# Attention, MoE and gated MLP in one kernel: the last token tile's logits with tokens in rows, its ranks from one-hot rows, the capacity branch ahead of the row loads, and full-size row transposes

## The chip, the cores and the metric

The kernel runs on one core of one Trainium2 chip. The metric is the device time of one execution in microseconds (us); the kernel before takes 963.38 us, the median of three runs (962.12 to 964.65). The core has five engines with a queue of instructions each: PE (TensorE, matrix products and transposes), DVE (VectorE), ACT (ScalarE), POOL (GpSimd) and SP (SyncE, which in this kernel issues nearly all DMAs). PE's weight loads have rows of their own in the profile (PEld). A "q" behind an engine's name (SPq, PEq, PEldq) marks what its sequencer does: branches, register loads, semaphore waits, DMA issues.

## The reference, cut to what matters

Three layers, each on the output of the one before. All inputs and outputs are fp32.

```python
# 1. attention: q, k, v (4, 8, 576, 64), s (4, 8, 576)
cum  = np.cumsum(np.maximum(s, 0), axis=-1)
sc   = q @ k.T / 8 + np.minimum(-(cum[:, :, :, None] - cum[:, :, None, :]), 0)   # causal mask
attn = exp(sc - max(sc)); out = attn / (sum(attn) + 1e-9) @ v
x    = out.transpose(0, 2, 1, 3).reshape(2304, 512)

# 2. mixture of experts: 8 experts, each token goes to one
logits     = normalised(x) @ normalised(expert_emb).T / tau
expert_idx = np.argmax(logits, axis=1); gate = softmax(logits)[token, expert_idx]
for e in range(8):
    out[expert_idx == e] = gate * (np.maximum(x[expert_idx == e] @ w1[e], 0) @ w2[e])   # 512 -> 1024 -> 512

# 3. gated MLP: w_a, w_b (512, 1536), w_out (1536, 512)
return ((out @ w_a) * (out @ w_b)) @ w_out
```

## The kernel before, in words

**Attention.** There are 4 batches with 4 head pairs each, so 16 units. `att` is a pool that holds this stage's buffers; `class Sched` is a planner that merges several streams of work items (scores, transposes of the exponentials, products with V, and the token-tile items below) into one order for PE by estimated due times, and puts the DVE, ACT and POOL operations (`V.push`, `V.chain`) where its model of each engine has room. What it emits is a fixed order for each engine; at run time each engine only waits on semaphores.

**Token tiles.** The 2304 tokens are 20 tiles (`NT`), five for each batch: four of 128 tokens and one of 64 tokens; in the last batch the 64-token tile is number 19, the last of all. For each tile three kinds of items follow each other. `x_item` forms the raw logits (before the softmax denominators are applied) for each head with the experts in rows (L857, the result `lp`, copied to `lt`), transposes the attention output so that tokens are in rows (L862), takes the reciprocal `r` of the denominators (L880, L887) and scales the rows (L895, the result `x`). `l_item` transposes `lt` back to tokens in rows (L930), scales it by `r` (L938, `lw`), sums over the heads (L947, `lg`), takes the maximum and its index (L950, L953), and forms the one-hot row `oh` (L956). POOL adds `oh` to a running count `sc` (L961). `r_item` gets each token's rank within its expert: a matmul of `oh` with a triangle matrix `ltri` (L982) and a matmul of the counts of the earlier tiles with `ones` (L983); DVE picks the rank (L989, L995) and makes the target row `sl` (L998), and POOL scatters the tile's rows into the DRAM buffer `xs`, sorted by expert (L1004). Ahead of the last `r_item` and behind the count matmul stand small matmuls with no use but to keep PE running (`warm`, L174): 28 and 30 of them (`WARM[5]`, `WARM[2]`).

**Counts.** Behind the last tile PE sums `sc` (L1250), and DVE sorts the experts by their counts: a chain of some 15 small operations from L1257 on. L1268 finds by how much the largest expert exceeds its capacity, and L1274 casts all these numbers to the integers `ci` that the sequencers load as registers. Each expert slot has a capacity in rows (`CAPS`: 352 for slot 0, and between 272 and 368 for the others).

**Between the stages.** The order from here on is written out by hand:

```python
            xload(0)
            wload2()
            for _ in range(4):
                misc.pop(0)()
            cbase[1] = nc.sync.value_load(ci[:1, 1, 1:2], min_val=0, max_val=N)
            ...                                     # 30 warm matmuls
            most = nc.values_load(ci[:1, 2, 0:1], min_val=-CAP, max_val=N)
            overflow()
            zfill(1)
```

`xload(0)` (L1332, L1333) loads slot 0's rows from `xs` into `xg`; it waits for all scatters. `misc` is a list of small DVE and ACT steps (the gate, output positions) that nothing needs until the end of the expert stage. `overflow` is a block for tokens beyond the capacity: all five engines compare `most` with zero and jump over it (L1661) when no expert overflows, as is the case here. `zfill(e)` (L1215) writes zeros into the part of `xs` that slot e's load reads beyond its rows, and `zero(xs[:CAPS[0]])` does that for slot 0 at the start of the kernel.

**Experts.** For each of the eight slots, eight steps f of 128 hidden columns: 12 matmuls `h` (L1510), then 12 matmuls `y` (L1535) for the step before. Each operand is split into a high and a low part, so three products make one. In steps 3 to 6 the next slot's rows are transposed for the next pass (`xtr`, L1361; for slot 0 `xtr0`, L1345): three transposes in each of four groups, and the third covers only the rows beyond 256 (96 rows for slot 0, 112 for slot 1, 88 and 72 for slots 2 and 3, then 40, 32, 32 and 16). `xload(e)` and `zfill(e)` run one slot ahead, on SP. Results go to `yt`.

**Third layer.** Six groups of 384 tokens. `yload(i)` (L1580) loads a group from `yt` into the same `xg` buffer, `ysplit` splits it (L1587, L1588), `tick` (among others L1433, on POOL) splits its weights, and `abmm` (L1600) and `omm` (L1621) are the products.

## Time and profile before

| | kernel before |
|---|---|
| median of 3 runs | 963.38 us (962.12 to 964.65) |
| the profiled execution | 960.65 us, its span 959.0 us |
| PE busy | 925.7 us, 97% of the span |
| DVE, ACT, POOL busy | 514.6, 432.8 and 255.1 us (54%, 45%, 27%) |
| mean granted TensorE clock | 0.994 |
| DMA | 107.90 MB, mean 113 GB/s |

The span is the time from the first to the last instruction; 1.65 us of the profiled execution lie outside it. Attention runs until about 258 us of the span, the stretch between the stages from there to 273 us, the experts to about 490 us, and the third layer to the end. A granted clock of 1.00 is 2.4 GHz, one of 0.50 is 1.2 GHz.

### The profile page before, as it was taken

Reading aid. Unit: us, or ns where it says so; the run is one execution under the profiler, and the core shown is the slowest. Engines: PE = TensorE matmul, PEld = TensorE weight load, DVE = VectorE, ACT = ScalarE, POOL = GpSimd, SP = SyncE. Lnnn points to the kernel's source line nnn. Section 1 sums busy time; section 2 is a strip of 40 time slices with the busy share of each in tenths; the row PEclk is TensorE's granted clock in tenths of the full one; section 3 lists DMA queues with packets and bytes.
Section 4 is the critical chain, followed back from the end, with each engine's and each line's share of the span. In section 5 each row is a group of like instructions: output and inputs, shape, how many; then the busy total and the mean of one; then the engine's idle time right before and its main releaser. Section 6 shows DMA issues by size and latency. Waiting matters only on the chain.

```text
span 959.0 us, 17720 instructions
## 1 busy us (share of the span) xinstructions
PE 925.7 (97%) x6471; PEld 846.6 (88%) x6472; DVE 514.6 (54%) x1319; ACT 432.8 (45%) x1075; POOL 255.1 (27%) x311
## 2 busy tenths in 40 slices
PE   8999999999889999999999999999999999999996
PEld 7777778777779999999998999999999999999995
DVE  8688889798764334444558888742222212222112
ACT  6677788876745444455544444432211211211111
POOL 6122323256223333344302433642001001001001
PEclk9999999999999999999999999999999999999999
DMA  4774555526286667667645443613010010000000
GB/s 130 172 155 110 137 119 124 139 71 183 72 254 227 225 192 231 201 211 222 190 156 166 132 132 119 108 18 100 1 33 34 1 33 33 1 1 33 1 1 33
DMA packets 102243, 107.90 MB, mean 113 GB/s; under 512 B 58429, under 2 KB 72717, under 8 KB 102141
## 3 DMA queue, kind: packets, MB, share of 16 engines
q1 hardware_dynamic: 98557, 97.04, 36.2%
q0 software_dynamic: 3552, 9.46, 2.8%
q8 instruction: 65, 1.06, 0.5%
q14 instruction: 37, 0.30, 0.1%
q10 hardware_dynamic: 32, 0.04, 0.0%
HBM read 77.90 MB, written 20.44 MB: 103 GB/s over the span
## 4 chain that ended last, share of the span: by engine, by line
PE 66%; DVE 2%; DMA 2%; issue 1%; ACT 0%; POOL 0%; POOLq 0%; SPq 0%; DVEq 0%; ACTq 0%
PE h L1600 15%; PE x L1600 15%; PE y L1621 13%; PE h L1510 11%; PE y L1535 10%; PE x L1361 1%; DMA xg<-xs 1%; PE x L1621 1%; PE h L1621 1%; DMA xg<-yt 1%; DVE cv L262 0%; DVE cv L265 0%; DVE mx L1611 0%; DVE w L1433 0%; DVE xl L1588 0%
## 5 line engine op out<-in xcount | busy, mean ns | idle before, releaser
L1611 DVE TENSOR_TENSOR mx<-x,mx 128x384 f32<-128x384 f32 x72 | 40.0, 556 | 220.0 <-PE x L1600 220.0
L1612 ACT CAST hh<-mx 128x384 fp32r<-128x384 f32 x71 | 36.4, 513 | 161.1 <-DVE mx L1611 161.1
L1606 ACT COPY mx<-h 128x384 f32<-128x384 f32 x72 | 34.6, 481 | 144.1 <-PE h L1600 144.1
L650 ACT ACTIVATE z<-z,mn 128x192 f32<-128x192 f32 (+3 forms) x128 | 78.2, 611 | 37.8 <-DVE mn L644 37.2
L1640 POOL DMA_INDIRECT out_dram<-mx,pmt x18 | 17.6, 979 | 291.0 <-DVE mx L1639 221.7
L1600 PE MATMUL x<-xh,w 128*128 128x384 f32 x288 | 79.0, 335 | 1.0 <-POOL w L1433 1.0
L1600 PE MATMUL h<-xh,w 128*128 128x384 f32 x288 | 79.7, 337 | 0.0
L1600 PE MATMUL h<-xh,v 128*128 128x384 f32 x288 | 79.7, 337 | 0.0
L630 PE MATMUL st<-KS,QS 128*128 128x288 f32 (+3 forms) x160 | 58.6, 374 | 8.9 <-DVE mn L644 7.5
L738 PE MATMUL pt<-ident,z 128*128 128x128 f32 x448 | 63.4, 277 | 3.2 <-ACT pT L180 1.6
L1519 DVE SCALAR_TENSOR_TENSOR hl<-h,hh 128x288 fp32r<-128x288 f32 (+6 forms) x64 | 31.2, 488 | 65.1 <-ACT hh L1518 65.1
L280 POOL TENSOR_TENSOR w<-st,w 128x512 fp32r<-128x512 f32 (+1 forms) x41 | 44.5, 1093 | 74.2 <-ACT w L272 48.9
L644 DVE CUSTOM_DVE_ANT_0 z<-st,maskb 128x192 f32<-128x192 f32 (+3 forms) x128 | 58.7, 478 | 9.5 <-PE st L633 7.6
L782 PE MATMUL xa<-pT,vn 128*64 128x128 f32 x896 | 61.2, 282 | 0.8 <-ACT pT L180 0.4
L1613 DVE TENSOR_TENSOR hl<-mx,hh 128x384 fp32r<-128x384 f32 x71 | 39.7, 559 | 41.1 <-ACT hh L1612 41.1
L1621 PE MATMUL y<-v,hh 128*128 128x512 f32 x192 | 59.8, 392 | 0.0
L280 POOL TENSOR_TENSOR v<-st,v 128x512 fp32r<-128x512 f32 x32 | 42.9, 1341 | 63.3 <-ACT v L272 53.0
L738 PEld LDWEIGHTS pt<-ident,z 128*128 128x128 f32 x448 | 49.8, 141 | 11.0 <-ACT z L650 4.3
L1510 PE MATMUL h<-xh,v 128*128 128x256 f32 (+2 forms) x256 | 59.2, 305 | 0.0
L1510 PE MATMUL h<-xh,w 128*128 128x288 f32 (+3 forms) x256 | 58.9, 306 | 0.0
L1535 PE MATMUL y<-hh,v 128*128 128x256 f32 (+2 forms) x256 | 58.1, 300 | 0.0
L782 PEld LDWEIGHTS xa<-pT,vn 128*64 128x64 f32 x896 | 49.1, 139 | 9.9 <-issue 5.7
(299 smaller groups left out, 2525.7 us busy)
## 6 DMA issues: line engine op xcount, KB each, us to landing
st<-in_moe_w_dram SPq DMA_DIRECT2D x64, 512.0 KB
QS<-sp SPq DMA_DIRECT2D x62, 128.0 KB
st<-in_moe_w_a_dram SPq DMA_DIRECT2D x12, 512.0 KB
st<-in_moe_w_b_dram SPq DMA_DIRECT2D x12, 512.0 KB
st<-in_moe_w_out_dram SPq DMA_DIRECT2D x12, 512.0 KB
xg<-yt SPq DMA_DIRECT2D x6, 768.0 KB
xg<-xs SPq DMA_DIRECT2D x8, 512.0 KB
kn<-in_k_dram SPq DMA_DIRECT2D x24, 128.0 KB
```

The lines of the kernel that those rows point to most:

```text
L280: e.tensor_tensor(out=o[:, 1, a:b], in0=t[:, a:b], in1=o[:, 0, a:b].bitcast(F32), op=ALU.subtract)
L630: nc.tensor.matmul(st[:m, :wp], lhsT=qs[:, h, s0 - 64:s0 - 64 + m], rhs=ks[:, h, c0:c0 + wp], start=True, stop=False)
L644: nc.vector.tensor_tensor_reduce(out=z[:m, h, c0:c0 + w], in0=st[:m, :w], in1=maskb[:m, S - kk + c0:S - kk + c0 + w], op0=ALU.add, op1=ALU ...
L650: nc.scalar.activation(out=z[:m, h, :kk], in_=z[:m, h, :kk], func=AF.Exp, scale=-1.0, bias=m1, accum_out=rsum[:m, tid(b, c), 2 * p + h:2 * ...
L738: nc.tensor.transpose(out=pt[:, 128 * x:128 * x + 128], in_=zs[i][:, h, a0:a0 + 128] if c else z0s[u % 2], identity=ident)
L782: nc.tensor.matmul(xa[64 * h:64 * h + 64, :m], lhsT=v_[:m, 2 * p + h, :], rhs=locs[i][bk, h], start=bk == 0, stop=bk == c,)
L1510: nc.tensor.matmul(ph[:, :n], lhsT=w[:, hl, 128 * f:128 * f + 128], rhs=mv[:, d, :n], start=k_ == 0, stop=k_ == 11,)
L1535: nc.tensor.matmul(ys[e][d][:, :n], lhsT=w[:, hl, c0 + 128 * d:c0 + 128 * d + 128], rhs=mv[:, :n], start=f == 0 and k_ == 0, stop=f == 7 a ...
L1600: nc.tensor.matmul(p, lhsT=w[:, hl, d, c0:c0 + 128], rhs=mv[:, d, :], start=d == 0 and k_ == 0, stop=d == 3 and k_ == 2,)
L1611: nc.vector.tensor_tensor(out=g, in0=pp[1], in1=g, op=ALU.mult)
L1613: nc.vector.tensor_tensor(out=gl, in0=g, in1=gh.bitcast(F32), op=ALU.subtract)
L1621: nc.tensor.matmul(ots[i][t], lhsT=st[:, 128 * t:128 * t + 128], rhs=w[:, hl, c0:c0 + 512], start=f == 0 and k_ == 0, stop=f == 11 and k_ ...
```

## The change

1. **The last tile's logits.** For tile 19 the logit matmul takes the operands the other way round, so that `lp` comes with tokens in rows. The copy to `lt` and the transpose back (L930) fall away. Its reciprocals `r` are pushed as soon as the last four units' sums are there, and the scaling of its rows (`fx`) is pushed only behind its one-hot row.
2. **Ranks of the last batch.** POOL's running count stops at tile 15. The ranks of tiles 15 to 19 and the final count are sums of one matmul on `sc` and one on each earlier one-hot row of the batch.
3. **Branch ahead of the row loads.** DVE casts the overflow number by itself into a new tile `cov`, directly behind L1268; the sequencers load it and take the branch before `xload(0)` is issued. `xload(0)` is three DMAs instead of two. The four `misc` steps, three operations that sort the bases (`eq`, `base`) and the low parts of three weight tiles move behind the branch.
4. **Fewer warm matmuls.** 10 instead of 28 ahead of the last ranks, and 2 ahead of the branch plus 3 behind it instead of 30; these five read their operands as plain fp32 (before: the split type fp32r).
5. **Full-size transposes.** All row transposes take 128 rows, whatever the slot's rows are; for slot 0 the unused rows of the tile are set to zero.
6. **Third layer's start.** `yload(0)` is issued behind step (6, 7) instead of (7, 1); in the last slot a `tick` also runs at step 5, with another argument from step 4 on.
7. **Zeros for slot 0.** `zero(xs[:CAPS[0]], 0)` leaves the list `pend` and is emitted at the scheduler's step 14.

How this moves instructions is shown at three places. First DVE at the last tile (line numbers of after are some 34 higher here: L938, L947, L956, L895 are L972, L981, L990, L919). Before:

```order
L956 TENSOR_SCALAR oh<-iota_85,ixs 128x8
L880 TENSOR_SCALAR r<-rsum_76 64x4 x2
L887 RECIPROCAL r<-r 64x8
L989 TENSOR_TENSOR jk<-pt,oh 128x8
L895 TENSOR_TENSOR x<-pt,r 64x512
L995 TENSOR_REDUCE rk<-jk 128x1
L938 TENSOR_TENSOR lw<-pt,r 64x64
L998 SCALAR_TENSOR_TENSOR sl<-ixs,rk 128x1
L947 TENSOR_REDUCE lg<-lw 64x8
L950 MAX mx<-lg 64x8
L953 MAX_INDEX ixs<-mx,lg 64x8
L956 TENSOR_SCALAR oh<-iota_85,ixs 64x8
```

After:

```order
L990 TENSOR_SCALAR oh<-iota_85,ixs 128x8
L972 TENSOR_TENSOR lw<-pt,r 64x64
L981 TENSOR_REDUCE lg<-lw 64x8
L1031 TENSOR_TENSOR jk<-pt,oh 128x8
L984 MAX mx<-lg 64x8
L1037 TENSOR_REDUCE rk<-jk 128x1
L987 MAX_INDEX ixs<-mx,lg 64x8
L1040 SCALAR_TENSOR_TENSOR sl<-ixs,rk 128x1
L990 TENSOR_SCALAR oh<-iota_85,ixs 64x8
L919 TENSOR_TENSOR x<-pt,r 64x512
L1031 TENSOR_TENSOR jk<-pt,oh 128x8
L1037 TENSOR_REDUCE rk<-jk 128x1
```

The last tile's `lw` now stands directly behind tile 18's `oh`, and the scaling of its rows (`x`) behind its own `oh`.

Second SP, from the last weight load of the attention stage to the branch and what follows it. Before:

```order
L1332 DMA xg<-xs 128x2x512
L1333 DMA xg<-xs 96x512
L242 DMA st<-in_moe_w_dram 128x2x512
L1711 TENSOR_LOAD ci
L1711 ISA x2
L1320 TENSOR_LOAD ci
L1320 ISA x2
L1719 TENSOR_LOAD ci
L1719 ISA x2
L1661 COMPARE_AND_BRANCH
```

After, the part up to the branch, and then the part where the branch lands:

```order
L243 DMA st<-in_moe_w_dram 128x1024
L243 DMA st<-in_moe_w_dram 128x2x512 x4
L1760 TENSOR_LOAD cov
L1760 ISA x2
L1704 COMPARE_AND_BRANCH
```

```order
L1704 UNCONDITIONAL_BRANCH
L1372 DMA xg<-xs 128x512 x2
L1372 DMA xg<-xs 96x512
L1763 TENSOR_LOAD ci
L1763 ISA x2
L1356 TENSOR_LOAD ci
L1356 ISA x2
L1257 ISA
L1257 DMA xs<-zrow 736x1x256
```

The loads of slot 0's rows (`xg<-xs`) and two register loads have moved from ahead of the branch to behind it, in front of the zero fill (`xs<-zrow`).

Third SP at the end of the expert stage, around the first load of the third layer's rows (`xg<-yt`) and the last slot's register load (`ci`) and result stores (`yt<-mx`). Before, where that load stands behind several of the last slot's stores:

```order
L1547 DMA yt<-mx 128x288
L1494 UNCONDITIONAL_BRANCH
L1547 ISA
L1547 DMA yt<-mx 128x288
L248 DMA st_8900<-in_moe_w_out_dram 128x1024
L1580 DMA xg<-yt 128x4x384
```

After:

```order
L249 DMA st_8730<-in_moe_w_b_dram 128x2x512
L1623 DMA xg<-yt 128x4x384
L1537 UNCONDITIONAL_BRANCH x2
L249 DMA st_8792<-in_moe_w_b_dram 128x2x512
L1586 TENSOR_LOAD ci
L1586 ISA x2
L1537 UNCONDITIONAL_BRANCH
L1590 REGISTER_ALU
L1590 DMA yt<-mx 128x288
```

That load now stands ahead of the last slot's register load and of all its stores.

The diff, cut to its core:

```diff
-WARM = (30, 84, 30, 0, 20, 28)
+WARM = (30, 84, 2, 0, 20, 10, 3)
...
+                        n0[0] += u > last - NP
+                        if n0[0] == NP:
+                            rlast[0] = sm.tile([128, H], F32, name="r")
+                            ...
+                            V.push(t, "D", 560, f3)
...
+                        if t == NT - 1:
+                            nc.tensor.matmul(lp[:m, 32 * p:32 * p + 32], lhsT=xw, rhs=ew, start=True, stop=True)
+                        else:
+                            nc.tensor.matmul(lp[32 * p:32 * p + 32, :m], lhsT=ew, rhs=xw, start=True, stop=True)
...
+                        if t < NT - 5:
+                            V.push(t_, "G", 163, f7, lambda t2: setattr(ot, "t", t2))
...
-                    nc.tensor.matmul(rp[:, :w], lhsT=ltri, rhs=oh[:, o, :].rearrange("p t e -> p (t e)"), start=True, stop=False)
-                    nc.tensor.matmul(rp[:, :w], lhsT=ones, rhs=sc[:, o, :].rearrange("p t e -> p (t e)"), start=False, stop=True)
+                    a = min(t0, NT - 5)
+                    nc.tensor.matmul(
+                        rp[:, :w], lhsT=ones, rhs=sc[:, a:a + k_, :].rearrange("p t e -> p (t e)"), start=True, stop=False
+                    )
+                    for x in range(a, t0):
+                        nc.tensor.matmul(rp[:, :w], lhsT=ones, rhs=oh[:, x, :], start=False, stop=False)
+                    nc.tensor.matmul(rp[:, :w], lhsT=ltri, rhs=oh[:, o, :].rearrange("p t e -> p (t e)"), start=False, stop=True)
...
             nc.vector.max(out=over, in_=key)
+            nc.vector.tensor_copy(out=cov, in_=over[:1])
...
+                if e == 0:
+                    for a in range(3):
+                        m = min(128, CAPS[0] - 128 * a)
+                        behind("xs", nc.sync.dma_start(out=t[:m, a], in_=xs[128 * a:128 * a + m, :]))
+                    return
...
-                    m = min(128, cap - 128 * a)
                     nc.tensor.transpose(
-                        out=pt[:, 128 * a:128 * a + m], in_=xgs[e][:m, a, 128 * d:128 * d + 128], identity=ident[:m, :m]
+                        out=pt[:, 128 * a:128 * a + 128], in_=xgs[e][:, a, 128 * d:128 * d + 128], identity=ident
                     )
...
+            w = slots[0, 0][:, 0, :].bitcast(F32)
...
+            wload2()
+            idle(WARM[2])
+            most = nc.values_load(cov[:1, 0:1], min_val=-CAP, max_val=N)
+            overflow()
             xload(0)
-            wload2()
-            for _ in range(4):
-                misc.pop(0)()
             cbase[1] = nc.sync.value_load(ci[:1, 1, 1:2], min_val=0, max_val=N)
             who(1)
...
+            idle(WARM[6])
             count(0)
-            most = nc.values_load(ci[:1, 2, 0:1], min_val=-CAP, max_val=N)
-            overflow()
+            for j in range(4, 7):
+                for x in range(2):
+                    lo_op("DG"[j == 6], wstate[j], slots[0, j], 512 * x, 512 * x + 512)
+            for _ in range(2):
+                misc.pop(0)()
             zfill(1)
...
-                    if (e, f) == (E - 1, 1):
+                    if (e, f) == (E - 2, 7):
                         yload(0)
...
-                        for _ in range(TICKS[0] if f not in (4, 5, 6) else 0):
-                            tick(5 if f < 7 else 3)
+                        for _ in range(TICKS[0] if f not in (4, 6) else 0):
+                            tick(5 if f < 4 else 3)
```

`idle(n)` runs n `warm` matmuls of 512 columns.

## Rows read from the trace of the kernel before

**Rows 1.** Page: chain of work that ended last, share of the span by engine
```profile
PE 66%; DVE 2%; DMA 2%; issue 1%; ACT 0%; POOL 0%; POOLq 0%; SPq 0%; DVEq 0%; ACTq 0%
```

**Rows 2.** Timeline of PE: start us, us, engine line op tile xcount [idle before <-releaser]
```profile
55.50 0.88 PE L782 MATMUL xa<-pT,vn 128*64 128x128 f32 x12 [0.43 <-ACT pT L180]
...
270.21 1.06 PE L1345 MATMUL y<-ident,xg 128*128 128x128 f32 x8 [2.90 <-PEq L1661]
...
285.96 0.41 PE L1361 MATMUL x<-ident,xg 128*128 128x128 f32 x2 [0.27 <-DMA xg<-xs]
286.53 0.31 PE L1361 MATMUL x<-ident,xg 112*128 112x112 f32 x1 [0.15 <-DMA xg<-xs]
...
489.31 0.39 PE L1535 MATMUL y<-hl,v 128*128 128x256 f32 x1 [0.94 <-DVE hl L1519]
...
525.87 0.62 PE L1600 MATMUL x<-xh,w 128*128 128x384 f32 x2 [0.97 <-POOL w L1433]
```

**Rows 3.** Line L1661, the branch: durations ns min/median/max, first to last start us
```profile
L1661 SPq EVENT_SEMAPHORE  x9: 17/17/17, 270.1 to 270.7; - x9
...
L1661 PEldq COMPARE_BRANCH  x1: 5480/5480/5480, 264.4 to 264.4; - x1
L1661 SPq COMPARE_BRANCH  x1: 50/50/50, 266.5 to 266.5; - x1
```

**Rows 4.** Windows: stretch, us, busy PE PEld DVE ACT POOL, clock, DMA share, GB/s
```profile
265.00:266.00 1.00, 1.00 (x6) 0.82 (x5) 1.00 (x2) 0.00 (x0) 0.00 (x0) 1.00 1.03 369
...
273.10:275.90 2.80, 2.80 (x12) 2.80 (x13) 0.67 (x3) 0.48 (x2) 0.00 (x0) 0.50 0.89 185
```

**Rows 5.** Chain in order of time, expert stage: start us, us, what, instructions
```profile
278.03 8.45 DMA xg<-xs
...
290.06 0.32 PE x L1361 x3
290.37 1.60 PE h L1510 x12
291.97 1.58 PE y L1535 x12
...
377.61 0.40 PE x L1361 x3
378.01 2.01 PE h L1510 x12
380.02 1.82 PE y L1535 x12
...
468.97 0.38 PE x L1361 x3
469.35 1.63 PE h L1510 x12
470.98 1.44 PE y L1535 x12
```

**Rows 6.** Timeline of DVE, last tile to the overflow number
```profile
256.38 0.30 DVE L956 TENSOR_SCALAR oh<-iota,ixs 128x8 bf16<-128x8 f32 x1
...
257.82 0.20 DVE L938 TENSOR_TENSOR lw<-pt,r 64x64 f32<-64x64 f32 x1
...
258.82 0.22 DVE L956 TENSOR_SCALAR oh<-iota,ixs 64x8 bf16<-64x8 f32 x1
...
259.33 0.17 DVE L989 TENSOR_TENSOR jk<-pt,oh 128x8 f32<-128x8 f32 x1 [0.29 <-PE pt L983]
...
261.59 0.17 DVE L1268 MAX8 pk<-jk 128x8 f32<-128x8 f32 x1
```

**Rows 7.** Line L1711, SP's load of one register, columns as in rows 3
```profile
L1711 SPq TENSOR_LOAD <-ci x1: 494/494/494, 264.4 to 264.4; - x1
```

**Rows 8.** Timeline of SP, the next DMA behind the branch
```profile
271.14 0.66 SPq L1215 DMA_DIRECT2D xs<-zrow  x1
```

**Rows 9.** Timeline of ACT, first use of the third layer's rows
```profile
485.25 0.51 ACT L1587 CAST xh<-xg 128x384 fp32r<-128x384 f32 x1 [2.32 <-DMA xg<-yt]
```

More of the change, by code (lines that the diff above doesn't have):

```diff
@@ L206, in moe_kernel @@
         ci = rt.tile([1, 5, E], I32, name="ci")
+        cov = rt.tile([1, E], I32, name="cov")
         tie = rt.tile([128, E], F32, name="tie")
@@ L598, in start @@
                             pend.pop(0)()
+                if i == 14:
+                    zero(xs[:CAPS[0], :], 0)
                 if wq and i >= 5 * 12:
@@ L705, in th1, with th2, f3 @@
                         rel.t = t
-                        V.push(t, "A", 0.833 * 64 + 280, f2, lambda t2: setattr(et, "t", t2))
+                        V.push(t, "A", 0.833 * 64 + 280, f2, th2)
+                    def th2(t):
+                        et.t = t
+                        n0[0] += u > last - NP
+                        if n0[0] == NP:
+                            rlast[0] = sm.tile([128, H], F32, name="r")
+                            def f3(_):
+                                for h in range(2):
+                                    first_r(rlast[0], B - 1, h)
+                                nc.vector.reciprocal(out=rlast[0][:64], in_=rlast[0][:64])
+                            V.push(t, "D", 560, f3)
                     V.push(end, "D", 1.042 * 64 + 77, f1, th1)
@@ L838, in tid, with first_r @@
                 return 5 * b + (4 - c if b == B - 1 else c)
+            rlast, lend = [None], [None]
+            def first_r(r, b, h):
+                nc.vector.tensor_scalar(
+                    out=r[:64].rearrange("p (a h) -> p a h", h=2)[:, :, h],
+                    in0=rsum0[64 * h:64 * h + 64, NP * b:NP * b + NP],
+                    scalar1=1e-9, scalar2=None, op0=ALU.add,
+                )
             def x_item(b, c):
@@ L928, in emit @@
                     x, r, lt = rts[t]
-                    lp = ps_t.tile([128, 512], F32, name="pt")
-                    nc.tensor.transpose(out=lp[:m, :128], in_=lt[:, :m], identity=ident)
-                    rel = Tok()
-                    pts.append(rel)
+                    if t == NT - 1:
+                        lp, (rel, more) = lt, lend[0]
+                    else:
+                        lp = ps_t.tile([128, 512], F32, name="pt")
+                        nc.tensor.transpose(out=lp[:m, :128], in_=lt[:, :m], identity=ident)
+                        rel = Tok()
+                        pts.append(rel)
                     lw = sm3.tile([128, H, E], F32, name="lw")
@@ L1249, in moe_kernel @@
             pt = ps_t.tile([128, 512], F32, name="pt")
-            nc.tensor.matmul(pt[:, :E], lhsT=ones, rhs=sc[:, NT, :], start=True, stop=True)
+            nc.tensor.matmul(pt[:, :E], lhsT=ones, rhs=sc[:, NT - 5, :], start=True, stop=False)
+            for t in range(NT - 5, NT):
+                nc.tensor.matmul(pt[:, :E], lhsT=ones, rhs=oh[:, t, :], start=False, stop=t == NT - 1)
             sbase, scnt, over, perm, more = (pk[:, x] for x in range(5))
@@ L1460, in m5 @@
             def m5():
+                eq = gp.tile([128, E, E], F32, name="eq")
+                nc.vector.tensor_tensor(
+                    out=eq, in0=perm.unsqueeze(1).to_broadcast([128, E, E]),
+                    in1=iota8.unsqueeze(2).to_broadcast([128, E, E]), op=ALU.is_equal,
+                )
+                nc.vector.tensor_tensor(out=eq, in0=eq, in1=sbase.unsqueeze(1).to_broadcast([128, E, E]), op=ALU.mult)
+                nc.vector.tensor_reduce(out=base, in_=eq, axis=AX.X, op=ALU.add)
                 nc.vector.tensor_tensor(out=lt, in0=oh, in1=base.unsqueeze(1).to_broadcast([128, NT, E]), op=ALU.mult)
```

68 lines of the change are left out of this document (29 added, 39 removed).

## The prediction

> **What bounds the kernel now.** PE is busy 97% of the span, and the page's chain of work that ended last [rows 1] is two thirds PE; DMA and DVE have 2% each. So a time can be won in two ways only: PE has less to do, or a gap of PE goes. I read the timeline of PE next, for its idle times [rows 2]. Behind the attention stage there are four places: 2.90 us ahead of the first row transpose at 270.21, put down to PE's own sequencer at L1661, the capacity branch; 0.27 and 0.15 us at slot 1's transposes at 285.96, for the rows from `xs`; 0.94 us at 489.31; and 0.97 us at 525.87. The line of the branch [rows 3] shows what a branch costs there: PE's record at 264.4 lasts 5480 ns; SP's record lasts 50 ns, but its next event stands 3.6 us later, at 270.1, and the last of its nine semaphore events at 270.7. The windows [rows 4] show the DMA engines full at that time (369 GB/s, share 1.03), and PE at half its clock (0.50, that is 1.2 GHz) from 273.1 to 275.9, at the first products behind the gap. The chain in order of time [rows 5] shows two more things. The 8.45 us from 278.03 are the load of slot 1's rows, on the path to the gap at 285.96. And the row transposes cost more than their own 0.3 to 0.4 us: the `h` group behind them is longer too.
>
> **Full-size transposes (−4.1 us).** In [rows 5] the group at 347.12, whose third transpose has 72 rows, takes 0.28 us, and the `h` group behind it 1.89 where a plain group of this slot takes 1.84: 0.33 in all. The first group with 40 rows (377.61) takes 0.40, its `h` 2.01 against 1.82 behind it: 0.59. The last, with 16 rows (468.97): 0.38, and 1.63 against 1.44, so 0.57. There are 16 such groups (slots 4 to 7, with 40, 32, 32 and 16 rows), all on the path since PE is full there. A transpose of 72 rows costs no step, one of 40 does: with 128 rows I expect the 0.33. The saving is between 0.24 and 0.26, and some 16 × 0.255 = 4.1 us. The more columns cost next to nothing: 0.28 us is for 72 rows, 0.32 at most if each row beyond costs as much as those within. Bounds: 0, if the dearer step has another cause than the row count, to −4.2.
>
> **The stretch between the stages (−1.3 us).** Worked along the path that ends at slot 1's rows.
> Last tile [rows 6]: `lw` stands at 257.82 and now directly behind tile 18's `oh` of 256.38, so at about 256.57, and `oh` of tile 19 follows 1.0 to 1.2 us later, at 257.75 instead of 258.82. The scaling of its rows, some 0.6 us, then stands on DVE between this `oh` and the rank picks; PE's rank matmuls run beside it, for which DVE waited about 0.3 us before. So the count chain begins some 0.8 us earlier, the overflow number is there at 260.8 instead of 261.59, and `cov`, one small cast, at 261.0. The five matmuls more in the ranks and in the count are short and stand where 18 warm ones fall away.
> Branch: one register load takes 0.49 us [rows 7], with its checks 0.9 to the next. SP now loads one ahead of the branch, so it branches at about 261.9 instead of 266.5 [rows 3]. Before, the time from SP's branch to the next DMA issue, the zero fill at 271.14 [rows 8], was 4.6 us: 3.6 of waiting, some 0.6 of semaphore events and the setting up. Now the same wait meets fewer loads, since slot 0's rows are issued behind it and only weights ahead. No row shows it without load: the bounds are 0.5 us (the branch record and nothing more) and 5.5 (PE's record). I take 3.15, a little under SP's own; with the semaphores the row loads are issued at 265.75.
> Rows: 352 rows of 2 KB at 369 GB/s take 2.0 us; with the latency and a weight load of 512 KB in the queue (1.4 us at that rate) I put the landing 4.0 us behind the issue. Only then may the zero fill of slot 1 go, at 269.8 instead of 271.14: −1.3. From there the chain is as before (zero fill, slot 1's row loads, 8.45 us), so slot 1's rows arrive 1.3 us earlier.
> PE has to be there as early. Before, it waited for the branch until 269.9 (264.4 and 5.48) and started at 270.21. Now it branches at about 262 and, with a wait of 4 to 5.5 us, returns at 266 to 267.5; the three fp32 warm matmuls of 512 columns come then. No row has such a one; they cost 3 × 0.25 us if they run as the fp32r ones do, and 3 × 0.9 if fp32 goes in four passes. So PE is free at 269 to 270, when the rows land. The second pass of transposes no longer waits for DVE, whose `misc` steps come later, and the 0.42 us of gaps at 285.96 are left as slack. That covers the −1.3; if PE's clock drops already in the warm matmuls, some 0.9 of it are lost. Range of this part: −4.4 (wait of 0.5) to +1.0 (wait of 5.5).
> What moves behind the branch (two `misc` steps, the `eq` operations, the low parts of the weights) goes to DVE and POOL, which are busy half and a quarter of the span; the low parts are needed only by the later products of slot 0, so I cost them at nothing. If that cover is gone, PE waits some tenths of a us at slot 0's fifth weight tile.
> Here the Trainium skill speaks against the value that I took. Advanced Engine Details and Errata, Control Flow Timing, gives about 108 ns for a compare-and-branch. PE's record is fifty times as long, so I don't follow it; by it the sum would be near the lower bound above. Runtime: NRT & Kernel Launch, Instruction fetch mechanics, says that a taken branch out of the loaded pages forces a DMA fetch; the 3.6 us of [rows 3] beside full DMA engines agree with it.
>
> **Third layer's start (−1.9 us).** At 485.25 ACT waits 2.32 us for the third layer's rows `xg<-yt` [rows 9]; behind that wait stand the casts of the last slot's hidden columns, for which DVE's `hl` and then PE wait at 489.31 (0.94), and weight splits, for which PE waits at 525.87 (0.97) [rows 2]. With `yload(0)` issued ahead of the last slot's stores the rows are there, and the additional `tick` at step 5 takes one weight split forward. I take both gaps: −1.9. Bounds: −0.5 (half of one goes, since a new tick on ACT and POOL stands in the same place) to −1.9.
>
> **Zeros for slot 0 and the rest (−0.4 us).** The zero fill leaves SP's queue ahead of the next unit's loads. PE's gap of 0.43 us at 55.50, at the first use of `vn` [rows 2], stands behind such a load: I take it, with bounds 0 and −0.4. Fewer copies, one transpose less and no running count on POOL in the last batch are beside PE's work and cost nothing.
>
> **The rivals.**
> Quick branch: without the row loads in front the wait is 0.5 us. Then the middle part gives −4.4, in all −10.8: 952.6. Only the 50 ns of SP's own record speak for it; the 5480 ns of PE speak against it [rows 3].
> Slow branch: the wait is 5.5 us, for the weights alone fill the queues. Middle part +1.0, in all −5.4: 958.0.
> The gaps of the third layer stay: the ticks' order and not the load sets them. In all −5.8: 957.6.
> The change doesn't do what it says: the dearer step is not the row count's. In all −3.6: 959.8.
> Slower, by the clock: PE now has 5 warm matmuls where it had 30 and is idle from about 262 to 266 and more, where it had run until 267. Before, after an idle time of 2.90 us, half speed followed for at least 2.8 us [rows 2, 4]. If half speed now lasts through four of slot 0's steps, it costs the time of these once more: a step is 24 matmuls of 288 columns, 2 × 1.44 us at least as in slot 6 [rows 5], so 4 × 2.9 = 11.5, and 967.2. It decides from some 11 us on, that is when nearly all four are slow. The one stretch seen is short, and PE then has work without a pause, which speaks against it. The Trainium skill, TensorE: Matmul & The Clock Gate, Why this matters for your kernels, warns of idle gaps between bursts of matmuls for the same reason; the 0.50 of [rows 4] agrees.
>
> **How the numbers follow.** −4.1 − 1.3 − 1.9 − 0.4 = −7.7 us. The profiled execution took 960.65, so 952.95; the median of the runs is 2.73 above it, at 963.38, so 955.7 for the median of the changed kernel. Chances: forecast 0.60 (its own range 953.7 to 957.7), quick branch 0.09, slow branch 0.12, third layer's gaps stay 0.09, row count not the cause 0.06, clock 0.04. The range takes in all but the last, with the spread of the runs: 952.3 to 959.9. A measurement of this kernel can tell about 0.3%, 2.9 us, from no change: faster means below 960.5, slower above 966.3. Of the cases all but the last two lie well below 960.5; with the row count's case near the edge and several misses at once that makes 0.89 faster, 0.07 the same and 0.04 slower.
>
> **What would show it.** Right: transposes of slots 4 to 7 with groups of 0.33 us in all instead of 0.57 to 0.59; no gaps at the last `y` groups and at the third layer's first products; the zero fill of slot 1 issued 1 to 2 us earlier, and SP's first event behind the branch some 3 us after it. Wrong: `h` groups behind the transposes still 0.2 us longer; SP or PE standing at the branch for 5 us and more; a granted clock of 0.50 in the windows of slot 0's products for more than 5 us; or a new gap of PE in slot 0, at weight tiles whose low parts now come later.

## The result, and the profile after

The changed kernel takes 954.96 us (median of 4 runs, 953.78 to 956.2) where the kernel before takes 963.56 (962.12 to 964.65): a ratio of 0.9912, 95% interval 0.9894 to 0.993. The prediction was 955.7 with a range of 952.3 to 959.9. The profiled execution of the changed kernel takes 953.78 us with a span of 952.1, so 6.9 us less than that of before (span 959.0); the medians lie 8.6 us apart, since the profiled execution of before is 2.7 us under its median and that of after 1.2 us.

| | before | after |
|---|---|---|
| median | 963.56 us | 954.96 us |
| span of the profiled execution | 959.0 us | 952.1 us |
| PE busy | 925.7 us | 917.8 us |
| mean granted TensorE clock | 0.994 | 0.994 |

That is not the whole result. The experiments below ran on two chips on which the kernel before takes 968.2 and 970.6 to 971.0 us (which chip the first measurement ran on is not on record). On the second of them the changed kernel, repeated twice, was no faster than before (1.001 and 0.9995); on the first it was not run itself. Where its gain went, and how it comes back, is the second half of the experiments.

The timeline of PE after, at the places of [rows 2]; columns as there:

```profile
54.12 0.88 PE L800 MATMUL xa<-pT,vn 128*64 128x128 f32 x12 [0.43 <-ACT pT L180]
...
251.22 0.66 PE L800 MATMUL xa<-pT,vn 128*64 128x128 f32 x8 [1.14 <-ACT pT L180]
...
264.54 3.63 PE L174 MATMUL h<-w 128*128 128x512 f32 x4 [2.84 <-PEq L1704]
...
268.89 1.37 PE L1382 MATMUL y<-ident,xg 128*128 128x128 f32 x8
...
284.27 0.41 PE L1397 MATMUL x<-ident,xg 128*128 128x128 f32 x2 [1.25 <-DMA xg<-xs]
285.00 0.33 PE L1397 MATMUL x<-ident,xg 128*128 128x128 f32 x1 [0.32 <-DMA xg<-xs]
...
503.00 0.44 PE L1643 MATMUL h<-xh,w 128*128 128x384 f32 x1 [1.25 <-ACT mx L1649]
```

The gaps of 0.94 and 0.97 us in the third layer are gone, and one of 1.25 has come at 503.00. The gap at slot 1's transposes has grown from 0.42 to 1.57 us. The gap of 0.43 at the use of `vn` is still there, 1.38 us earlier in the span.

The chain of waits in order of time, after: start us, us, what, instructions.

```profile
266.21 3.38 DMA xg<-xs
...
269.80 6.20 DMA xs<-zrow
...
276.73 8.23 DMA xg<-xs
...
376.08 0.33 PE x L1397 x3
376.40 1.79 PE h L1553 x12
378.19 1.79 PE y L1578 x12
...
463.65 0.33 PE x L1397 x3
463.98 1.44 PE h L1553 x12
465.42 1.44 PE y L1578 x12
```

The groups of slots 4 to 7 have lost their step: 0.33 us and nothing in the `h` group behind, where [rows 5] have 0.40 with 2.01 against 1.82, and 0.38 with 1.63 against 1.44. The stretch between the stages ends in three DMAs one behind the other: the last of slot 0's row loads, the zero fill, and the last of slot 1's row loads.

The line of the branch after, columns as in [rows 3]:

```profile
L1704 SPq EVENT_SEMAPHORE  x9: 17/17/17, 263.8 to 264.4; - x9
...
L1704 PEldq COMPARE_BRANCH  x1: 3402/3402/3402, 260.8 to 260.8; - x1
...
L1704 SPq COMPARE_BRANCH  x1: 50/50/50, 261.1 to 261.1; - x1
```

**Ledger of the two profiled executions**, from the start times of the same instructions:

| stretch | before | after | won in it | forecast |
|---|---|---|---|---|
| start to tile 18's one-hot row on DVE (L956, now L990) | 256.38 | 255.54 | 0.84 | 0.4 |
| from there to the third transpose for slot 1 | 286.53 | 285.00 | 0.69 | 1.3 |
| from there to the first plain `h` group behind the last transposes | 472.42 | 466.86 | 4.03 | 4.1 |
| from there to the last result's operation on DVE | 950.80 | 943.92 | 1.32 | 1.9 |
| sum | | | 6.88 | 7.7 |

The 0.84 of the first line isn't the change's own. At the same PE instructions, PE ran at half its clock in the profile of before and at full clock after (windows: stretch, us, busy PE PEld DVE ACT POOL, granted clock, DMA share, GB/s). Before:

```profile
28.00:29.00 1.00, 1.00 (x12) 1.00 (x10) 0.48 (x2) 0.69 (x2) 0.00 (x0) 0.50 0.24 57
```

After:

```profile
28.00:29.00 1.00, 1.00 (x21) 0.85 (x16) 0.68 (x3) 0.69 (x2) 0.00 (x0) 1.00 0.82 177
```

The code is the same there, and in five of the profiles of experiments with the changed attention part the clock is 0.50 there too. It gave 1.38 us by 54 us of the span; 0.54 of it were lost again up to the last tile, where after has a wait of 1.14 us at 251.22 and before, at another operation, one of 0.71. Without this stretch the change's own gain in the profile is some 5.5 us (an estimate, 6.88 less 1.38).

### The profile page after: what moved, and what is told of

Same layout as the page of the kernel before. It is cut to its first block, busy times and chain, and to the rows that moved or that the text cites. A ratio compares the mean times of both kernels' runs of the same rounds, so it can differ in the third digit from the quotient of the medians.

```text
span 952.1 us, 17669 instructions
## 1 busy us (share of the span) xinstructions
PE 917.8 (96%) x6447; PEld 839.7 (88%) x6448; DVE 516.9 (54%) x1319; ACT 432.0 (45%) x1074; POOL 256.4 (27%) x308
## 4 chain that ended last, share of the span: by engine, by line
PE 68%; DMA 2%; DVE 0%; issue 0%; SPq 0%; POOLq 0%; ACT 0%; DVEq 0%; ACTq 0%
PE h L1643 16%; PE x L1643 16%; PE y L1664 14%; PE y L1578 10%; PE h L1553 10%; DMA xg<-xs 1%; PE x L1397 1%; PE x L1664 1%; PE h L1664 1%; DMA xs<-zrow 1%; DMA yt<-mx 0%; DVE xl L1631 0%; SPq L1372 0%; POOLq L1878 0%; DVE mx L1654 0%
## 5 line engine op out<-in xcount | busy, mean ns | idle before, releaser
L281 POOL TENSOR_TENSOR w<-st,w 128x512 fp32r<-128x512 f32 (+1 forms) x43 | 47.1, 1101 | 68.1 <-ACT w L273 57.8
```

The source lines that it names most:

```text
L281: e.tensor_tensor(out=o[:, 1, a:b], in0=t[:, a:b], in1=o[:, 0, a:b].bitcast(F32), op=ALU.subtract)
```

## The experiments

The theory to be tested was the prediction's sum: the row count of the transposes, the branch ahead of the loads, the third layer's start. Each kernel ran beside the kernel before on its chip. The first four shared a chip on which before takes 968.18 us (29 runs).

**Row count, undone in the changed kernel.**

```diff
+                    m = min(128, cap - 128 * a)
                     nc.tensor.transpose(
-                        out=pt[:, 128 * a:128 * a + 128], in_=xgs[e][:, a, 128 * d:128 * d + 128], identity=ident
+                        out=pt[:, 128 * a:128 * a + m], in_=xgs[e][:m, a, 128 * d:128 * d + 128], identity=ident[:m, :m]
                     )
```

> The changed kernel with one part undone: the transposes of slots 1 to 7 take only the rows beyond 256 again. Theory, a transpose of few rows brings a step of its own: the 16 groups of slots 4 to 7 cost 0.57 to 0.61 us each in all again instead of 0.33 (transposes plus what the h group behind them takes beyond a plain one), so 4.0 us more than the changed kernel, about 959.0. Rival, the step belongs to something else that the change also moved (the order of the weights or the banks): the groups stay at 0.33 and the time at 955.

Measured: 974.05 us, 1.0058 of before (1.0036 to 1.0081). The chain in order of time at the last transposes of this kernel:

```profile
476.68 0.38 PE x L1398 x3
477.06 1.63 PE h L1554 x12
478.69 1.44 PE y L1579 x12
```

The group costs 0.57 us again (0.38, and 1.63 against 1.44). From the first transposes of slot 4 to the last of slot 7 this kernel takes 91.2 us, the kernel before 91.4 and the changed kernel 87.6. So the mechanism holds to 0.2 us. The whole time doesn't fit: 4 us more than a changed kernel that is 7 to 8 us faster than before would still be faster than before. Its profile shows where the rest was lost: from the first plain `h` group behind the last transposes to the last result it takes 486.8 us, where the first profile of the changed kernel takes 477.1 and the next experiment's kernel, on this chip, 480.9. The later groups look for the reason.

**Row count alone, in the kernel before.**

```diff
-                    m = min(128, cap - 128 * a)
                     nc.tensor.transpose(
-                        out=pt[:, 128 * a:128 * a + m], in_=xgs[e][:m, a, 128 * d:128 * d + 128], identity=ident[:m, :m]
+                        out=pt[:, 128 * a:128 * a + 128], in_=xgs[e][:, a, 128 * d:128 * d + 128], identity=ident
                     )
...                                              # and slot 0's transposes (xtr0) likewise
```

> The kernel before with one part of the change alone: all row transposes take 128 rows. Theory of the row count: 963.6 less 4.0, about 959.5, groups of slots 4 to 7 at 0.33 us in all. Rival, the step belongs to something else: 963.6. If the parts of the change don't add up (a gap comes back elsewhere), this one wins less than 4.0.

Measured: 964.92 us, 0.9967 (0.9949 to 0.9985), so 3.3 us less than before, with 4.0 inside the interval of 1.5 to 4.9. Slots 4 to 7 take 87.6 us as in the changed kernel. This part of the gain is there on a chip with longer times too.

**The branch behind the row loads again.**

```diff
+            xload(0)
             wload2()
             idle(WARM[2])
+            cbase[1] = nc.sync.value_load(ci[:1, 1, 1:2], min_val=0, max_val=N)
+            who(1)
             most = nc.values_load(cov[:1, 0:1], min_val=-CAP, max_val=N)
             overflow()
-            xload(0)
-            cbase[1] = nc.sync.value_load(ci[:1, 1, 1:2], min_val=0, max_val=N)
-            who(1)
```

> The changed kernel with the capacity branch behind slot 0's row loads and the two register loads again; the overflow number, the five warm matmuls and all else stay. Theory of the prediction, the branch waits longer when row loads are queued ahead of it: SP's wait behind the branch 3.5 us or more, PE's 5 us or more, and 1.3 us more in all, about 956.3. Rival, the part was won by the shorter chain of the last tile alone, and the place of the branch is worth nothing or costs: the row loads leave about 3 us earlier than in the changed kernel, SP's branch stands near 264, the zero fill of slot 1 near 268.7 instead of 269.80, and the time is the same or up to 1 us less, 954.0 to 955.0.

Measured: 971.76 us, 1.0035 (1.0017 to 1.0053); the whole time again holds a loss in the third layer (484.4 us, counted as above, where the next experiment's kernel takes 479.9), so the place of the branch is read from its own stretch. The timeline of SP in this kernel:

```profile
271.60 1.73 SPq L1372 DMA_DIRECT2D xg<-xs  x3
280.15 0.65 SPq L1257 DMA_DIRECT2D xs<-zrow  x1
```

Counted from tile 18's one-hot row on DVE (at 264.21 here, 261.73 in the next experiment, which has the branch in front, and shares the chip), the row loads leave after 7.4 us instead of 11.0, but the zero fill, which stands behind the branch, after 15.9 in both, and slot 1's third transpose comes after 30.3 and 30.6. So on this chip the place of the branch is worth nothing: what the loads win in front of it, the branch loses behind them. The kernel of the experiment above, which has the order of before with the row counts changed alone, takes 31.5 us for the same stretch: 0.9 to 1.2 us are won on this chip too, with either place of the branch. The waits themselves, 4.3 us from SP's branch (275.9) to the zero fill here against 3.7 to the row loads in the first profile of the changed kernel, differ by 0.6 us where the prediction had 0.75. PE's record is 3.36 us with the row loads ahead and 3.40 without: row loads ahead of the branch don't bring back the 5.48 of before.

**The third layer's start undone.**

```diff
-                    if (e, f) == (E - 2, 7):
+                    if (e, f) == (E - 1, 1):
                         yload(0)
...
-                        for _ in range(TICKS[0] if f not in (4, 6) else 0):
-                            tick(5 if f < 4 else 3)
+                        for _ in range(TICKS[0] if f not in (4, 5, 6) else 0):
+                            tick(5 if f < 7 else 3)
```

> The changed kernel with the first load of the third layer's rows at step (7, 1) again, and the weight splits (ticks) of the last slot as before. The two traces say: two gaps of 0.94 and 0.97 us went and one of 1.25 came (ACT waits for a result store), net 0.66: so 0.7 us more, about 955.6. The prediction's term: 1.9 more, 956.9. Rival, the gap of 1.25 is due to another part of the change, then it stays and the two come back: 956.9 with three gaps.

Measured: 964.82 us, 0.9967 (0.995 to 0.9984). Its timeline of PE:

```profile
491.46 0.39 PE L1578 MATMUL y<-hl,v 128*128 128x256 f32 x1 [1.28 <-DVE hl L1562]
...
511.71 0.44 PE L1643 MATMUL h<-xh,w 128*128 128x384 f32 x1 [1.07 <-ACT mx L1649]
```

The first of the two old gaps is back, larger (1.28): the earlier row load takes it away. The gap of 0.97 is not back, so its going belongs to another part of the change; which one isn't settled. The wait for `mx`, where ACT waits for a store of the last slot's result, stays with 1.07. It isn't tied to this part either, nor to the kernel: one of the two repeats of the changed kernel below has 0.85 us there and the other nothing.

More was in this run than its place. Between 600 and 660 us of the span (columns as in the windows above), the kernel with the row counts undone:

```profile
600.00:660.00 60.00, 53.82 (x262) 48.87 (x261) 31.36 (x49) 18.23 (x36) 26.80 (x24) 0.91 0.24 54
```

and this one, on the same chip:

```profile
600.00:660.00 60.00, 59.16 (x313) 55.30 (x312) 34.96 (x56) 21.97 (x43) 32.10 (x29) 1.00 0.38 82
```

PE is idle for 6.2 us in the first, and for 6.4 us in the kernel with the branch behind the row loads (clock 0.97), but for 0.84 us with the old start of the third layer, as in the kernel before with full-size transposes (59.16 us busy as well). So on this chip the kernels that keep the new start of the third layer stand still for a time between 625 and 643 us, and the one that undoes it hardly does. No run repeats this on the other chip.

**The changed kernel itself, and three more, on a second chip** (before 970.96 us, 35 runs).

> The changed kernel itself once more, so that the other kernels of this group have it on their own chip. If the gain is the kernel's, 0.9912 of the time before again (0.989 to 0.993). Rival: on the chip of the first four experiments DVE waited 1.67 us at the rank pick of the last tile in every kernel with the changed last tile, and in none with the old; if that comes with the change, the ratio is nearer to 0.994.

Measured: 972.0 us, 1.001 (0.9991 to 1.003): nothing is left of the gain. The wait that I suspected explains about 1 us (DVE stands 0.84 us just ahead of tile 19's one-hot row, and PE 1.09 for that row). The large loss is elsewhere. The timeline of ACT of this run in the third layer:

```profile
628.23 0.51 ACT L1655 CAST hh<-mx 128x384 fp32r<-128x384 f32 x1 [8.03 <-issue]
...
636.85 0.48 ACT L1649 COPY mx<-h 128x384 f32<-128x384 f32 x1 [7.02 <-remote]
```

and that of PE:

```profile
628.25 0.45 PE L1643 MATMUL x<-xh,u 128*128 128x384 f32 x1 [3.00 <-issue]
```

ACT stands still twice, for 8 and 7 us, and PE for 3 us, in each case for nothing that the profile shows. Compared with the first profile (span 952.1 against 968.6), 6.3 us lie ahead of tile 18's one-hot row, 1.2 between there and slot 1's transposes, none in the experts, and 9.0 behind them. The first of these is mostly not the change's: on both chips the kernels built on the one before reach this row at 260.8, where the first profile of before has 256.38.

> The changed kernel, with the zero fill of slot 1 declared free of slot 0's row loads (their rows are disjoint), so that it isn't held until these have landed. Theory, the chain that ends the stretch between the stages runs from the row loads' landing (3.4 us) over the zero fill (6.2 us) to slot 1's row loads (8.2 us), and PE stands 1.57 us at its end (1.25 and 0.32): the fill leaves some 3 us earlier, the row loads of slot 1 some 2 us earlier, and both gaps go: 1.5 us less than the changed kernel on this chip. Rival, the zeros take the queues from the row loads, so the transposes of slot 0 start later by what is won: no change.

The edit puts slot 0's three row loads and the zero fill of slot 1 into a group without dependences among them:

```diff
-                        behind("xs", nc.sync.dma_start(out=t[:m, a], in_=xs[128 * a:128 * a + m, :]))
+                        x = nc.sync.dma_start(out=t[:m, a], in_=xs[128 * a:128 * a + m, :])
+                        behind("xs", x)
+                        tc.add_to_no_dep_group("z1", x.ins)
...
+                x = zero(xs[bass.ds(r + who(e) * RW, CAPS[e]), :], e)
+                if e == 1:
+                    tc.declare_no_dep(x.ins, group="z1", reason="rows of another slot")
```

Measured: 970.05 us, 0.9993 (0.9974 to 1.0012), 2 us under the changed kernel on this chip with intervals that overlap. In its profile the fill leaves 3.5 us behind the first row load instead of 4.7, and PE's three transposes for slot 1 stand without a gap:

```profile
291.00 0.49 PE L1401 MATMUL x<-ident,xg 128*128 128x128 f32 x3
```

Counted from tile 18's one-hot row, the third of them comes after 29.9 us instead of 30.7. So the chain of three DMAs was the end of that stretch, as the theory says; the 1.5 us can't be told from the noise of the whole time. What ends it now is PE: the windows show half speed while the three fp32 warm matmuls run,

```profile
272.00:277.00 5.00, 4.98 (x6) 2.06 (x7) 3.06 (x8) 0.00 (x0) 0.00 (x0) 0.50 0.48 147
```

and they take 5.5 us (from 272.02) where the repeat, at full clock, takes 2.8. So part of what the shorter chain wins goes to PE's clock.

> The changed kernel with the last tile's logits made as those of the other tiles (experts in rows, copy, transpose back, scaling of the rows ahead of the one-hot row). Theory, tile 19's one-hot row comes 1.1 us later (from tile 18's one-hot row to the last rank matmul 2.71 us before, 1.62 after) and everything up to slot 1's rows with it: 1.1 us more than the changed kernel. Rival, the scatter of the last rows or the branch sets the end and hides it: no change.

```diff
+LT = -1
...
-                        if t == NT - 1:
+                        if t == LT:
...
-                    end_ = t == NT - 1
+                    end_ = t == LT
...                                              # and the other places of the last tile likewise
```

Measured: 969.89 us, 0.9989 (0.9972 to 1.0007), so 2.1 us less than the changed kernel beside it where the theory had 1.1 more. Tile 19's one-hot row comes 2.63 us behind tile 18's instead of 2.02 in the repeated changed kernel and 1.14 in its first profile, but slot 1's third transpose comes no later (29.6 us behind tile 18's one-hot row, 30.7 in the repeat). DVE's wait of 0.84 us ahead of this one-hot row, which the repeat has, is missing here, and PE's warm matmuls at half speed end the stretch in place of the DMAs, so this run doesn't decide what the last tile's part is worth.

> The changed kernel with 30 short warm matmuls (fp32r) ahead of the branch and none behind it, as before. Theory, SP's chain and not PE ends the stretch, and where half speed falls on warm matmuls or on waiting it costs nothing: the same time within 1 us, or up to 1.7 us more if a stretch of half speed now falls on the first products. The rival of the prediction, too few warm matmuls hold the clock down: then this one is faster than the changed kernel by 1 us or more.

```diff
-WARM = (30, 84, 2, 0, 20, 10, 3)
+WARM = (30, 84, 30, 0, 20, 10, 0)
...
-            w = slots[0, 0][:, 0, :].bitcast(F32)
+            w = slots[0, 0][:, 0, :]
```

Measured: 971.64 us, 1.0008 (0.9993 to 1.0024), the same as the changed kernel beside it. Thirty short warm matmuls win nothing here, where the DMA chain ends the stretch (PE still waits 1.53 us for slot 1's rows).

**What stands still at 620 to 637 us.** At that time POOL issues 20 small scatters in a row (`pm<-pd,pos`, the output positions), and the engines stand without a releaser. The new theory: they wait for instruction blocks, which come by DMA and come late while these scatters run. The last group of kernels tests it, on the same chip (before 970.62 us, 16 runs).

```diff
-                if 16 <= k_ < 21:
-                    for t in range(4 * (k_ - 16), 4 * (k_ - 15)):
-                        m6(t)
...
+                    if 0 <= 8 * e + f - 8 < NT:
+                        m6(8 * e + f - 8)
```

The first three lines were in the third layer; the last two stand at the end of each step of the expert loop.

> The changed kernel, with the 20 small scatters of the output positions (POOL, pm<-pd, about 1 us each) not in a row in the third layer, where they stand at 609 to 641 us, but one behind each step of slots 1 to 3. In the repeated run of the changed kernel PE, ACT and DVE stood still at 620 to 637 us with no releaser of their own (ACT 8.0 and 7.0 us, DVE 5.8, PE 3.0 for issue), and the third layer was 9.5 us longer there than in the first profile of the same kernel. Theory, instruction blocks are fetched by DMA and come late while the scatters run: without them there the stall goes, and this kernel is 8 to 9 us faster than the changed kernel on a chip where that one stands still, 0 on one where it doesn't. Rival, the late block has nothing to do with the scatters: the stall stays at about 620 to 637, or moves by less than 10 us, and the time is that of the changed kernel.

> The changed kernel itself on the chip of this group. Theory, the gain of the change is 7 us (0.7%) wherever no engine stands still at 620 to 637 us, and nothing is left of it where they do: so either 0.991 to 0.994 of the time before with no such stall in its profile, or about 1.000 with it. Rival, the gain depends on something else of the chip: then stall and ratio don't go together.

Measured: the spread scatters 961.49 us, 0.9903 (0.9879 to 0.9927); the changed kernel beside it 970.5, 0.9995 (0.9971 to 1.0019). The windows of the two kernels, first the changed kernel:

```profile
600.00:660.00 60.00, 54.81 (x262) 50.20 (x261) 28.01 (x46) 17.17 (x34) 25.23 (x24) 0.91 0.22 50
```

then the one with spread scatters:

```profile
600.00:660.00 60.00, 60.00 (x319) 56.33 (x318) 32.59 (x52) 19.75 (x39) 10.75 (x9) 1.00 0.25 78
```

In 60 us the changed kernel does 262 matmuls and the other 319: PE is idle for 5.2 us, and runs at half its clock for a while behind that (mean 0.91, so some 4.9 us more, an estimate). That covers the 9.0 us between the medians, and it is gone when the scatters are moved. The DMA queues of the changed kernel between 626 and 636 us (queue, kind: packets, MB, share of 16 engines) show what else is there:

```profile
q14 instruction: 1, 0.01, 1.8%
q0 software_dynamic: 205, 0.01, 1.7%
q8 instruction: 1, 0.02, 0.6%
```

One instruction packet of 0.01 MB takes 1.8% of 16 engines for 10 us, that is 2.9 us, beside 205 packets of the scatters. In the kernel with spread scatters the long packets have moved to where the scatters now are; between 334 and 349 us two of them take 2.4% of 15 us, so 2.9 us each:

```profile
q8 instruction: 2, 0.03, 2.4%
```

But a long packet alone stops no engine here. PE is busy through these 15 us, and in the first profile of the changed kernel, between 617 and 622 us, a packet takes 2.6 us among the scatters with PE busy all the time:

```profile
q8 instruction: 1, 0.02, 3.3%
```

Nor does a slow packet cover the first wait: ACT stands from 619.0 to 627.1 in this second repeat, and between 602 and 627.5 us its DMA queues show no instruction packet at all, only these:

```profile
q1 hardware_dynamic: 812, 2.06, 32.4%
q0 software_dynamic: 448, 0.01, 1.3%
```

So this is shown: the stall goes when the scatters are moved. That the engines wait for instructions is not shown, and the scatters are not enough by themselves. With the same 20 in a row, PE has no gap longer than 0.84 us there in the kernels built on the one before, in the changed kernel with the old start of the third layer, or in its own first profile; and in the first profile of before two instruction packets among the scatters take only 0.3 and 1.0 us. Moving the scatters also shifts the instructions of the third layer, and no run moves the one without the other; which of the two counts stays open.

> The spread scatters and the zero fill of slot 1 that no longer waits for slot 0's row loads, together. Theory: the gain of the spread scatters plus 0.8 to 1.5 us, and PE's gaps at slot 1's first transposes (1.25 and 0.32 in the first profile of the changed kernel) gone. Rival, the zeros only take the place of something else: the same time as with the spread scatters alone.

Measured: 960.79 us, 0.9893 (0.9868 to 0.9917), the best of all on this chip: 9.8 us less than before and 9.7 less than the changed kernel. PE has no gap at slot 1's transposes. Against the spread scatters alone (961.49) the difference is not told from none.

**Where the row count's limit lies**, in the kernel before:

```diff
-                    m = min(128, cap - 128 * a)
+                    m = min(128, cap - 128 * a) if a < 2 or e < 4 else (64, 72, 96, 48)[e - 4]
```

> The kernel before with the third transpose of slots 4, 5, 6 and 7 on 64, 72, 96 and 48 rows (40, 32, 32 and 16 before); rows beyond the slot's own are left over from the slot before and are not used. Theory, the step comes with row counts of the smaller kind and its limit lies between 40 and 72: the groups (transposes plus what the h group behind them takes beyond a plain one) cost 0.33 us with 72 and 96, 0.57 to 0.60 with 48; 64 tells on which side the limit lies. Rival, the cost grows smoothly with fewer rows or belongs to the slots: four values in order, or all at 0.57.

Measured in a single run (968.6 us, too few to compare the whole time), the chain in order of time with 64, 72, 96 and 48 rows:

```profile
385.11 0.42 PE x L1361 x3
385.53 2.01 PE h L1510 x12
387.55 1.82 PE y L1535 x12
...
414.59 0.28 PE x L1361 x3
414.87 1.58 PE h L1510 x12
416.45 1.53 PE y L1535 x12
...
439.79 0.30 PE x L1361 x3
440.09 1.46 PE h L1510 x12
441.54 1.44 PE y L1535 x12
...
464.11 0.41 PE x L1361 x3
464.51 1.62 PE h L1510 x12
466.13 1.44 PE y L1535 x12
```

In all, with the `y` group as the plain one: 0.61, 0.33, 0.32 and 0.59 us. It is a step, with 64 rows still on the dear side and 72 on the cheap one. The Trainium skill, TensorEngine Tiling (Array Packing), Key Properties, says that a change of the tiling mode drains TensorE; a step between 64 and 72 rows, part of it in the `h` group behind, agrees with that; no row here shows the mode itself.

## Why the prediction was right, and where its steps were not

**The row count (4.1 forecast, 4.03 measured)** was right in size and cause. The prediction's 0.33 goes by a group at 347.12 that its rows 5 leave out; they hold the one at 290.06 with 112 rows, which costs 0.34 in the same way. The group it means is this, from the chain of the kernel before:

```profile
347.12 0.28 PE x L1361 x3
347.40 1.89 PE h L1510 x12
349.29 1.84 PE y L1535 x12
```

**The stretch between the stages (1.3 forecast, 0.69 measured).** SP's branch stands at 261.1 (forecast 261.9), the first row load at 264.81 (265.75), the zero fill at 269.80 (269.8). That the last agrees is luck: tile 18's one-hot row was 0.84 earlier for another reason, and the fill went 5.0 us behind the first row load, not 4.0. Two steps failed. The landing of the rows was put 1 us too short; from the last of the three loads alone it takes 3.38 us. And the step that gives the branch's place a gain has none: the experiment with the branch behind the loads reaches slot 1's transposes as early (30.3 against 30.6 us). Its own rival, that moving the loads costs what the shorter wait saves, was right. What won the 0.69 is argued and not shown: by the two profiles it is the shorter chain of the last tile (its one-hot row follows tile 18's after 1.14 us, not 2.44), but the experiment that undoes this chain doesn't decide it. The bound of -4.4 for a wait of 0.5 us doesn't follow from the terms either: 0.5 in place of 3.15 gives -1.3 - 2.65, so -4.0.

PE's share was sized well: the three fp32 warm matmuls take 2.8 us at full clock in the repeat, near the upper value of 3 × 0.9. In the profile after they run from 264.54 on (six records, the first four in 3.63 us, mostly at half speed) and end by 269.1; the transposes begin at 268.89 without a wait for the rows. The chain of three DMAs, not PE, set the end; the gap at 284.27 and 285.00 (1.57 us) is the slack that this left.

**The third layer's start (1.9 forecast, 1.32 measured).** Both gaps went, as forecast. By the start times of the same matmuls the first place won 1.20 us and the second 1.35, and a new wait took 1.23 of it: ACT's wait for the store of the last slot's result, 1.25 us at 503.00. For the first gap the mechanism is shown: with the old start it is back. For the second it failed: with the old start and the old ticks the 0.97 is not back, so something else in the change took it away, and that this part's sum came out near is in part luck. The wait that the prediction missed stands behind the stage that it looked at.

**Zeros for slot 0 (0.4 forecast).** Wrong in its cause: the gap of 0.43 stands unchanged at 54.12, and no gain comes from it. That the first line of the ledger shows 0.84 is the clock, and luck for the sum: without it the profile won less than the 7.7 forecast by some 2 us.

**The rivals.** Slower by the clock didn't happen in this profile: half speed falls on the warm matmuls and on waiting (windows of after: 0.50 from 264.7 to 268.0, full from 272). In seven of the ten profiles of the other kernels with the change it lasts longer, from 264 to 267 on until 277.5 to 280.9, over all warm matmuls and up to slot 0's first transposes, but it ends ahead of the slot's first products in each; where PE still waits for slot 1's rows behind it, this costs nothing. The quick branch and the slow branch are out by SP's 2.7 us to the first event. The way in which the change loses most of its gain was not among the rivals: a stall some 130 us behind the last place that the diff touches, the weight splits of the last slot, which end by 490 us. The first measurement's profile doesn't have it; both repeats have it. The prediction put no price on what the new start of the third layer does behind that layer's first products. The range holds the first measurement; it would not hold those repeats, and the 0.89 for faster was too sure for a gain of 0.9%.

## What to carry to other kernels

Look at the instruction behind a small transpose as well as at the transpose: with up to 64 rows each group cost some 0.25 us more, and padding it to full size took that away at no cost that shows. In a chain of DMAs that wait for each other only because the program can't tell their rows apart, undo the wait before reordering engines around it; here this took away PE's gap of 1.0 us behind the chain, though the whole time couldn't tell it from nothing. And repeat a gain of one per cent on a second chip before believing in it: there a stall beside a row of small scatters, at another place in the program, cost more than the whole change won, and spreading the scatters out gave 0.9% again.

## What the runs showed of the hardware

Three transposes of which the last has 64 rows or fewer, between matmuls on all rows, cost 0.24 to 0.28 us more than with 72, part of it in the matmuls behind. PE, ACT and DVE stood still for 3.0, 8.0 and 5.8 us with no releaser ("issue", "remote") while small scatters ran, and PE then ran at half its clock for a time; the same code in the same order showed it on one chip in both repeats and not in the first profile, and the cause is open. Among such scatters single instruction packets of 0.02 MB took 2.6 to 2.9 us in the changed kernels, where one in the kernel before took 1.0. A branch that is taken cost SP 2.7 to 3.6 us to its next event and PE 3.4 to 5.5, though its own record on SP is 50 ns.
